# Turning the first block's results per row tile, moving its own normalised rows, and cutting the warm-up products

## The chip, the cores and the metric

One core of one Trainium2 chip. The metric is the device time of one execution in microseconds (us), lowest is best. Each kernel is run several times; the median is quoted, and for comparisons the mean against the runs of the kernel before taken in the same rounds. Profiled executions come with a trace: TensorE products (PE), weight loads (PEld), VectorE (DVE), ScalarE (ACT), GpSimd (POOL), and the sync engine's queue (SPq), which issues most transfers.

## The reference, cut to what matters

```
xn = layernorm(x)                            # 2048 rows of 640
s  = attention(xn @ wq, k_cache, v_cache) @ wo
g  = silu( (sigmoid(xn @ w_gate) * (xn @ w_up)) @ w_down )     # 640 -> 1536 -> 640
out = x + s * g
```

The change lies in the part that makes `g`, in the first of four blocks of 512 rows. It touches no arithmetic.

## The kernel before

A block is four row tiles of 128 rows. The first block is done differently from the other three: as no data has arrived, it starts from single row tiles. Row tiles are centred, turned by TensorE itself, multiplied with the gate and up weights in three groups of 512 columns (`fg`), and the products end up in `h_row`, rows on partitions. The down projection wants them the other way round, in `hT`; four DMA transposes ("turns") do that.

```
        def norm_first(t):              # the first block's properly normalised rows,
            def step():                 # wanted only by the queries, much later
                normal(t)               # VectorE, writes xn
                turn_dma(t)             # DMA transpose xnT <- xn, in the sync queue
            return step

        dummy(18)                       # 18 products of 256 columns on zeros
        dummy(6, 64)                    # 6 of 64 columns
        stats_half(0, 0)                # the first real work, once x has landed
        ...
        steps = [norm_piece(1, i) for i in range(TQ + 1)]     # rows of the second block
        steps[TQ:] = [steps[TQ]] + [norm_first(t) for t in range(TQ)]
        k = 1
        for fg in range(1, F // FT):
            for t in range(TQ):
                tile_half(t, fg, k, 0)                         # gate products
                tile_half(t, fg, k, 1)                         # up products
                tile_gated(t, fg, k, steps.pop(0) if steps else None)   # -> h_row
                k = (k + 1) % 4
        hT[0] = hpool.tile([P, NF, TB], BF16, name="hT")
        for t in range(TQ):
            nc.sync.dma_start_transpose(hT[0][:, :, t * P:(t + 1) * P], h_row[:, t, :])
        while steps:
            steps.pop(0)()
        for b in range(1, NB):
            for f in range(2):
                gated(b, f, k)
                k = (k + 1) % 4
            for q in range(TQ):
                down(b - 1, q, k)       # wants hT of row tile q
            ...
```

In the traces below, the sync queue issues its transfers in the order of the program; waits on data come on top.

The softmax here doesn't subtract the row's maximum and nothing guards it: scores larger than these inputs give would overflow.

## Time and profile before

| | kernel before |
|---|---|
| median of the 3 runs known first | 922.86 us |
| lowest, highest | 922.26, 922.90 |
| span of the profiled core | 920.8 us |
| TensorE share of the chain that ended last | 98% |

TensorE is in work for nearly all of the span, so the reader should not look at shares but at the few places where two products are further apart than one product takes. The prediction below shows the profile's lines for this. One view it tells without showing is the sync queue around the first down projection, in order of time (start in us, duration in us, engine, line, operation):

```profile
28.95 5.32 SPq L241 DMA_TRANSPOSE xnT<-xn  x3
34.32 5.12 SPq L363 DMA_TRANSPOSE hT<-h_row  x3
```

Three turns of the first block's normalised rows (xnT) come before the first turn of results (hT), though row tile 0's results were ready at 28.37 us.

### The profile page before, as it was taken

The numbers are of one execution on the slowest core, as the hardware profiler recorded it, in microseconds if no ns is written. First come the engines' busy times: TensorE is split into PE (matmuls) and PEld (weight loads), VectorE is DVE, ScalarE is ACT, GpSimd is POOL, SyncE is SP. The second block draws the span as 40 slices with busy tenths as digits, with TensorE's granted clock in tenths as the row PEclk, the third lists the DMA queues.
The fourth block names the chain that finished last, engine by engine and source line by source line (L and its number), as shares of the span: only waits on it lengthen the run. The fifth ranks groups of instructions, "written<-read, shape, count | busy, mean of one in ns | idle before, by whom it ended". The sixth has DMA issues, their size and how long they took to land.

```text
span 920.8 us, 24985 instructions
## 1 busy us (share of the span) xinstructions
PE 915.1 (99%) x11340; PEld 623.3 (68%) x11340; DVE 493.7 (54%) x989; ACT 302.3 (33%) x332; POOL 134.1 (15%) x159
## 2 busy tenths in 40 slices
PE   9999999999999999999999999999999999999998
PEld 4445455466868686767676777777776767686875
DVE  6452522445646464645555555545564646464667
ACT  4222222255142424233333333242424151515150
POOL 1000100001002000200120011001100111166733
PEclk9999999999999999999999999999999999999999
DMA  9920330115344434342525162515251615273536
GB/s 320 154 53 1 89 86 1 43 62 88 74 67 106 87 56 84 93 98 42 98 80 112 36 104 79 113 32 109 64 108 47 113 61 90 67 113 110 95 73 138
DMA packets 172107, 79.35 MB, mean 86 GB/s; under 512 B 149953, under 2 KB 167569, under 8 KB 172001
## 3 DMA queue, kind: packets, MB, share of 16 engines
q1 hardware_dynamic: 164640, 55.85, 31.7%
q0 software_dynamic: 5808, 20.52, 7.8%
q8 instruction: 88, 1.44, 0.7%
q10 hardware_dynamic: 1552, 1.39, 0.5%
q14 instruction: 19, 0.15, 0.1%
HBM read 39.45 MB, written 2.62 MB: 46 GB/s over the span
## 4 chain that ended last, share of the span: by engine, by line
PE 98%; DVE 1%; DMA 0%; SPq 0%; ACT 0%; issue 0%; DVEq 0%
PE bank L518 22%; PE bank L447 21%; PE bank L469 19%; PE bank L429 18%; PE bank L251 8%; PE bank L263 6%; PE bank L293 3%; PE bank L395 1%; PE bank L194 0%; PE bank L553 0%; DMA hT<-h_row 0%; DVE gate L504 0%; DVE o_sb L499 0%; SPq L241 0%; PE bank L235 0%; DVE h_row L303 0%
## 5 line engine op out<-in xcount | busy, mean ns | idle before, releaser
L433 ACT ACTIVATE E<-bank 128x1024 bf16<-128x1024 f32 x256 | 255.3, 1022 | 456.7 <-PE bank L429 456.6
L447 PE MATMUL bank<-xnT,wq_sb 64*128 64x512 bf16 x1800 | 226.4, 376 | 0.0
L518 PE MATMUL bank<-wo_sb,oT 64*128 64x320 bf16 x2688 | 205.2, 296 | 0.0
L429 PE MATMUL bank<-qT,kT 64*128 64x512 bf16 x1536 | 200.7, 376 | 0.0
L469 PE MATMUL bank<-vbuf,E 64*128 64x193 bf16 x4096 | 195.3, 243 | 0.1
L469 PEld LDWEIGHTS <-E 64*128 64x128 bf16 x4096 | 178.8, 94 | 10.5 <-issue 0.7
L518 PEld LDWEIGHTS <-oT 64*128 64x128 bf16 (+1 forms) x2892 | 163.2, 94 | 30.7 <-issue 0.3
L454 DVE CAST qT<-bank 128x1024 bf16<-128x1024 f32 x90 | 110.2, 1224 | 128.5 <-PE bank L447 128.5
L447 PEld LDWEIGHTS <-wq_sb 64*128 64x128 bf16 x1800 | 106.1, 100 | 87.0 <-issue 0.4
L429 PEld LDWEIGHTS <-kT 64*128 64x128 bf16 x1536 | 88.2, 94 | 73.5
L482 DVE TENSOR_TENSOR o_st<-bank,rden 128x768 bf16<-128x768 f32 x128 | 122.5, 957 | 4.4
L533 DVE TENSOR_TENSOR acc<-bank,acc 128x640 f32<-128x640 f32 x96 | 79.0, 823 | 20.2 <-PE bank L518 20.2
L118 POOL DMA_DIRECT2D vbuf<-in_A_v_cache_dram x28 | 21.1, 753 | 310.7 <-PE bank L469 307.7
L452 DVE COPY seen<-bank 128x2 f32<-128x2 f32 x90 | 14.3, 159 | 79.1 <-PE bank L447 79.1
L481 DVE RECIPROCAL rden<-bank 128x4 f32<-128x4 f32 x128 | 23.4, 183 | 60.1 <-PE bank L469 59.1
L263 PE MATMUL bank<-wd_sb,hT 128*128 128x512 bf16 (+1 forms) x384 | 52.8, 299 | 0.5 <-DMA hT<-h_row 0.5
L263 PEld LDWEIGHTS <-hT 128*128 128x128 bf16 x384 | 29.6, 98 | 23.9 <-DMA hT<-h_row 1.0
L257 DVE TENSOR_TENSOR hT<-bank,sig 128x512 bf16<-128x512 f32 x36 | 24.8, 690 | 38.2 <-ACT sig L254 38.2
L251 PE MATMUL bank<-xnT,wg_sb 128*128 128x512 bf16 x180 | 44.7, 379 | 0.0
L251 PE MATMUL bank<-xnT,wu_sb 128*128 128x512 bf16 x180 | 44.7, 379 | 0.0
L254 ACT ACTIVATE sig<-bank 128x512 bf16<-128x512 f32 x36 | 21.5, 597 | 55.8 <-PE bank L251 52.7
L97 POOL DMA_DIRECT2D wq_sb<-in_A_wq_dram x7 | 6.3, 900 | 210.5 <-PE bank L447 210.5
(51 smaller groups left out, 408.4 us busy)
## 6 DMA issues: line engine op xcount, KB each, us to landing
wo_sb<-in_A_wo_dram SPq DMA_DIRECT2D x7, 960.0 KB, 5.6
wq_sb<-in_A_wq_dram POOLq DMA_DIRECT2D x7, 960.0 KB, 6.0
k_st<-in_A_k_cache_dram POOLq DMA_DIRECT2D x14, 384.0 KB, 5.4
vbuf<-in_A_v_cache_dram POOLq DMA_DIRECT2D x28, 192.0 KB, 3.4
row<-in_A_x_dram POOLq DMA_DIRECT2D x16, 160.0 KB, 3.4
oT<-o_st SPq DMA_TRANSPOSE x128, 3.5
x_sb<-in_A_x_dram SPq DMA_DIRECT2D x3, 640.0 KB, 9.5
wd_sb<-in_B_w_down_dram SPq DMA_DIRECT2D x1, 1920.0 KB, 14.0
```

Of the source, the lines that this page charges most:

```text
L251: nc.tensor.matmul(bank[k][:, half, 0:r1 - r0], lhsT=w[:, c, f * P:(f + 1) * P], rhs=xnT[:, b, c, r0:r1], start=(c == 0), stop=(c == NCD - 1))
L257: nc.vector.tensor_tensor(hT[b][:, f, r0:r1], bank[k][:, 1, 0:r1 - r0], sig[:, 0:r1 - r0], ALU.mult)
L263: nc.tensor.matmul(wide(k)[:, d0:d1], lhsT=hT[b][:, f, q * P:(q + 1) * P], rhs=wd_sb[:, f, d0:d1], start=(f == 0), stop=(f == NF - 1))
L293: nc.tensor.matmul(bank[k][:, half, :], lhsT=xcT[:, c, t * P:(t + 1) * P], rhs=w[:, c, fg * FT:(fg + 1) * FT], start=(c == 0), stop=(c == ...
L429: nc.tensor.matmul(bank[k][:, i, :], lhsT=kT[r, pr, j, c * P:(c + 1) * P], rhs=q[r, pr * DJ + j, :], start=(j == 0), stop=(j == DJ - 1))
L433: nc.scalar.activation(E[u, pr][:, c, :, :], bank[k][:], AF.Exp, scale=scale_qk)
L447: nc.tensor.matmul(bank[k][:, half, :], lhsT=wq[r, c, col:col + DJ * (P - 1) + 1:DJ], rhs=xnT[r, b, c, :], start=(c == 0 and not second), ...
L454: nc.vector.tensor_copy(qT[u][:, 2 * m:2 * m + 2, :], bank[k][:])
L469: nc.tensor.matmul(o4[:, q, 0:DH + 1], lhsT=e[r, c, h % 2, q * P:(q + 1) * P], rhs=vbuf[r, h, c, 0:DH + 1], start=(turn == 0 and qq == 0 a ...
L482: nc.vector.tensor_tensor(o_st[u][:, :, h * DH:(h + 1) * DH], o4[:, :, 0:DH], rden[:].to_broadcast([P, TQ, DH]), ALU.mult)
L518: nc.tensor.matmul(res[:, half, :], lhsT=oT[u][r, cc, q * P:(q + 1) * P], rhs=wo[r, cc, half * HD:(half + 1) * HD], start=(turn == 0 and c ...
L533: nc.vector.tensor_tensor(cols(acc[:, t, :]), res, cols(acc[:, t, :]), ALU.add)
```

## The change

Its intent: let the first down projection find its operand in place, and let the first real products start sooner.

```diff
-        dummy(18)
-        dummy(6, 64)
+        dummy(17)
...
-        steps[TQ:] = [steps[TQ]] + [norm_first(t) for t in range(TQ)]
+        hT[0] = hpool.tile([P, NF, TB], BF16, name="hT")
...
                 tile_gated(t, fg, k, steps.pop(0) if steps else None)
                 k = (k + 1) % 4
-        hT[0] = hpool.tile([P, NF, TB], BF16, name="hT")
-        for t in range(TQ):
-            nc.sync.dma_start_transpose(hT[0][:, :, t * P:(t + 1) * P], h_row[:, t, :])
-        while steps:
-            steps.pop(0)()
+                if fg == F // FT - 1:
+                    nc.sync.dma_start_transpose(hT[0][:, :, t * P:(t + 1) * P], h_row[:, t, :])
...
-                gated(b, f, k)
+                gated(b, f, k, norm_first(f) if b == 1 else None)
...
-                gated(b, f, k, norm_piece(b + 1, f - 4) if b + 1 < NB and f >= 4 else None)
+                between = norm_first(f) if b == 1 and f < TQ else None
+                if b + 1 < NB and f >= 4:
+                    between = norm_piece(b + 1, f - 4)
+                gated(b, f, k, between)
```

## The prediction

> **What bounds the kernel now.** I read the page first: its head, its busy line, and its chain of work that ended last.
>
> ```profile
> span 920.8 us, 24985 instructions
> ...
> PE 915.1 (99%) x11340; PEld 623.3 (68%) x11340; DVE 493.7 (54%) x989; ACT 302.3 (33%) x332; POOL 134.1 (15%) x159
> ...
> PE 98%; DVE 1%; DMA 0%; SPq 0%; ACT 0%; issue 0%; DVEq 0%
> ```
>
> The tensor engine carries 98% of the chain. No other engine is near it, so only two things can shorten this program: less work on that engine, or fewer stretches in which it stands still. The change touches neither the mathematics nor the later 880 us, so I looked for standing time. The view of who waited for whom, cut to the tensor engine, has three entries for the whole program:
>
> ```profile
> PE bank L194 <- DVE warm L169: 1.1, 1, 1.1
> PE bank L263 <- DMA hT<-h_row: 0.5, 1, 0.5
> PE bank L293 <- ACT xnT L237: 0.2, 1, 0.2
> ```
>
> The first is the start of the program, which stays. The second is the one wait the change aims at: the first down projection (L263) waits for the turned results of the first block (hT). The 0.5 us is counted from the modelled end of the product before; products follow each other at 0.216 us and overlap. The last up product starts at 37.27 us by the trace's start times and the first down product at 38.20, so the step is 0.92 us where 0.216 would do: the true loss is **0.71 us**. The chain in order of time, cut to 25 to 45 us, shows what made it:
>
> ```profile
> 31.21 0.70 ACT sig L300
> 31.91 0.02 issue
> 31.93 0.75 DVE h_row L303
> 32.68 0.37 DVE xn L218
> 33.05 0.02 issue
> 33.07 1.20 SPq L241
> 34.27 0.05 issue
> 34.32 3.83 DMA hT<-h_row
> 38.15 0.05 issue
> 38.20 6.91 PE bank L263 x49
> ```
>
> Columns are start, duration, what. The reader is to see that the turn of the first row tile was not waiting for its own data. It stood in the sync queue behind a turn of normalised rows (L241), which itself waited for VectorE to write those rows (L218) at 32.68. Then issue to landing takes 3.83 us.
>
> Last, the beginning, tensor engine alone:
>
> ```profile
> 3.59 1.81 PE L194 MATMUL bank<-warm 128*128 128x256 bf16 x12
> 5.21 0.51 PE L235 MATMUL bank<-ident,xn 128*128 128x128 bf16 x3
> 5.88 0.57 PE L293 MATMUL bank<-wg_sb,xnT 128*128 128x512 bf16 x1 [0.16 <-ACT xnT L237]
> 6.28 0.28 PE L235 MATMUL bank<-ident,xn 128*128 128x128 bf16 x2
> 6.39 1.24 PE L293 MATMUL bank<-wg_sb,xnT 128*128 128x512 bf16 x4
> 7.47 0.44 PE L235 MATMUL bank<-ident,xn 128*128 128x128 bf16 x5
> 7.75 0.81 PE L293 MATMUL bank<-wu_sb,xnT 128*128 128x512 bf16 x3
> ```
>
> The warm-up products (L194) run until the first real transpose at 5.21, but VectorE had the first 128 columns of centred row 0 ready at 4.35 + 0.26 = 4.61 us (its timeline). So the transpose waited about 0.6 us behind warm-up products that were queued ahead of it.
>
> **What the Trainium skill says.** "TensorE: Matmul & The Clock Gate", Part 1 (The HAM clock gate), says the array starts at half clock and needs a window of some 3.4 us of activity to get the full one, the window running freely against the kernel. The trace agrees about the half clock: warm-up products of 256 columns start 0.213 us apart, later ones of 512 columns 0.216 us apart, and the first gate product took 0.567 us where later ones take 0.379. By these durations the change came at about 6.2 us here, in spite of 18 + 6 warm-up products. The page's PEclk row doesn't show it. "Perfetto Trace Analysis", Identifying the Most-Contended Engine, warns that matmul busy share overstates how near a kernel is to its limit; so I used start-to-start gaps, not the 99%. "DMA: Bandwidth & Descriptors", Rules for kernel authors, advises issuing a transfer early and waiting late; the 3.83 us above, exposed only because issued late, agrees. The same page (Silent corruption: two transposing streams in flight at once) forbids transposes from two queues; all stay on sync, so no serialising wait is added. No run here shows that corruption.
>
> **The change, part by part.**
>
> *Turning each row tile when done.* No turn is added or removed: 4 of hT before and after. In the kernel before, the last group of columns of row tile 0 is written by VectorE (L303) at 27.62 + 0.75 = 28.37 us, of tiles 1, 2 and 3 at 30.5, 32.7 and 34.8. The order of the sync queue in the changed build is: four turns of the second block's rows, then the four hT turns, then the first block's normalised rows. The fourth of the former is issued at 27.66 and takes 1.2 us or so, so tile 0's turn can be issued at about 28.9 and, with 3.8 us to landing, be there at 32.7, against the 37.49 us at which the down projection could start. That is 4.8 us to spare. Tile 3 is issued at about 36.6 (tiles queue 1.8 us apart) and lands near 42.3 even at 5.7 us, the slowest of the four in the view of that tile, and is wanted only after three down projections of 3.3 us each, at about 47.4. **Gain 0.71 us**, all on the path.
>
> *Moving the four normalised rows.* Four VectorE operations of 0.44 us (L218) and four turns go from the last tiles into the first four gate groups of the second block. Nothing reads these rows until the query products (L395), over 100 us later. There VectorE has one product of 0.69 us in each 2.16 us group, so 0.44 more fits (1.13 of 2.16), with four banks rotating. **0 us.**
>
> *Warm-up products.* 17 of 256 columns in place of 18 of 256 and 6 of 64: 0.213 + 6 x 0.0535 = 0.53 us fewer at the head of the queue. The 17th ends its slot at 4.66, just after the 4.61 above. The first transpose moves from 5.21 to about 4.68. ScalarE's copy follows its end (0.30 us) and takes 0.28, so the first gate product goes from 5.88 to about 5.34. From there the trace's half clock counts: if the full clock still comes at 6.2, the transposes of chunks 3 and 4 start at 5.34 + 0.43 = 5.77 instead of 6.28, their copy (0.38 us) ends at about 6.6 rather than 6.97, and the fourth product starts at about 6.65 rather than 7.03: 0.38 us. If the full clock comes by 5.3, the whole 0.54. From there the engine runs in close order and the shift is carried to the end. I take **0.43 us**.
>
> Sum: 0.71 + 0.43 = 1.14 us, 922.86 - 1.14 = 921.7 us.
>
> **Rivals.** *The weights aren't there.* The DMA engines are full in these first microseconds, and an earlier tensor engine may only meet a transfer instead. Issue plus time to landing: first gate weights 1.18 + 4.1 = 5.28 us, wanted at 5.34; first up weights 2.13 + 5.0 = 7.13, wanted at 7.2 to 7.4 instead of 7.75; the other two up chunks 3.17 + 5.2 = 8.37, wanted at 9.0. All just in time. With transfers 0.3 us later the start would gain only 0.15: 922.0.
> *The clock comes later.* With less activity early, the full clock could slip by up to a window. Each 512-column product then takes 0.427 us (twice 0.213) instead of 0.216; a slip of 3.4 us, the skill's figure, costs half, an estimated 1.7 us: 923.4. Against it: only 0.53 us of work leaves, and real transposes and products move into that time. I give it one chance in ten. An earlier clock, by the same free window, is the lucky side: some 0.5 us better.
> *The wait moves.* The second block's gate products might wait if hT turns delayed its rows; but those four turns are ahead in the queue. Turns could slow each other: the DMA row of the first 45 us is at its 9s during the four hT turns. Spread over eight microseconds they have more room, and 4.8 us to spare. Value 922.4 if a wait of that size came back; unlikely.
> *Later slack swallows it.* The whole rest has two steps above 0.26 us between products (at 177 and 883 us), so nothing there waits on a fixed time.
>
> **Range and chances.** The three runs before spread 0.64 us. The start gives -0.4 to +0.6 on my sum in ordinary cases, the clock up to 1.7 in a rare one. Range 920.8 to 922.7. Two per cent is 18 us, out of reach of anything here but another state of the chip: faster 0.005, same 0.99, slower 0.005.
>
> **What would show it.** Right: no tensor wait on hT in the wait view, a step of 0.22 us before the first down product, no L303, L218 or sync pieces in the chain at 31 to 38 us; 11333 tensor products (7 fewer); first transpose near 4.7, first gate product near 5.3, the fourth near 6.65; everything after 40 us earlier by 1.1. Wrong: a first gate product later than 5.6 or a wait on the up weights (DMA rival); 0.567-like durations after 7 us (clock rival); a new wait at L251 near 33 us or at L263 near 38 (wait moved).

## The result and the profile after

The changed kernel took 921.75 us (median of 4 runs, 921.03 to 922.59), the kernel before 922.68 us (median of 4). A ratio here is the mean time of one kernel's fast runs over that of the other's of the same rounds, so not quite the ratio of the medians: 0.9991, with a 95% interval of 0.9973 to 1.0008. This interval holds 1, so these runs alone do not prove a gain. The same kernel in five more runs beside nine of the kernel before (run e8) gave 921.77 against 922.87 us, ratio 0.9987, interval 0.9974 to 0.9999. The predicted time was 921.7.

The traces say more than so small a difference of times can. The page of the changed kernel:

```profile
span 919.2 us, 24974 instructions
...
PE 914.1 (99%) x11333; PEld 622.8 (68%) x11333; DVE 492.5 (54%) x989; ACT 302.3 (33%) x332; POOL 134.6 (15%) x159
...
PE 99%; DMA 1%; DVE 0%; SPq 0%; DVEq 0%; issue 0%
```

Seven products fewer (x11333), VectorE and ScalarE with the same number of instructions, and ScalarE gone from the chain. Who waited for whom, TensorE alone (waiter, what it waited for: us in total, times, longest):

```profile
PE bank L194 <- DVE warm L169: 1.1, 1, 1.1
PE bank L293 <- DMA wg_sb<-in_B_w_gate_dram: 0.2, 1, 0.2
```

The wait of the down projection (L263) for hT is gone. A wait for the first gate weights has come in its place at the very start; the kernel before had there a wait for ScalarE's copy. The chain in order of time, 25 to 45 us:

```profile
24.95 7.77 PE bank L293 x36
32.72 4.32 PE bank L251 x20
37.04 8.09 PE bank L263 x59
```

Three pieces of products and nothing between, where the kernel before had ScalarE, VectorE, the sync queue and a transfer. The sync queue in the changed kernel:

```profile
25.24 3.54 SPq L241 DMA_TRANSPOSE xnT<-xn  x2
28.87 6.99 SPq L361 DMA_TRANSPOSE hT<-h_row  x4
35.95 2.87 SPq L241 DMA_TRANSPOSE xnT<-xn  x2
```

The first hT turn goes out at 28.87 us instead of 34.32. By the start times, the first down product now starts 0.216 us after the product before it, where it was 0.924: 0.708 us won. The beginning, TensorE alone:

```profile
4.54 0.48 PE L235 MATMUL bank<-ident,xn 128*128 128x128 bf16 x3
5.21 0.38 PE L293 MATMUL bank<-wg_sb,xnT 128*128 128x512 bf16 x1 [0.19 <-DMA wg_sb<-in_B_w_gate_dram]
5.43 0.27 PE L235 MATMUL bank<-ident,xn 128*128 128x128 bf16 x2
5.54 1.24 PE L293 MATMUL bank<-wg_sb,xnT 128*128 128x512 bf16 x4
6.62 0.44 PE L235 MATMUL bank<-ident,xn 128*128 128x128 bf16 x5
7.14 0.81 PE L293 MATMUL bank<-wu_sb,xnT 128*128 128x512 bf16 x3
```

The first transpose moved from 5.21 to 4.54 us, the first up product (last line) from 7.75 to 7.14: 0.61 us won in this execution. But it was an execution in which everything went well: the first gate product took 0.38 us, so the full clock was there already (the warm-up products turned from 0.213 us apart to 0.11 apart at about 4.1 us). And the chain of this start no longer comes from the tensor engine:

```profile
2.13 4.96 DMA wu_sb<-in_B_w_up_dram
7.10 0.04 issue
7.14 2.53 PE bank L293 x11
```

The first up product waited for its weights, which landed at 7.10 us. So two questions were left: is each of the two gains what it seems, and what sets the start of the program?

### The profile page after: what moved, and what is told of

Read it like the earlier page. It is cut to its first block, busy times and chain, and to the rows that moved or that the text cites. A ratio compares the mean times of both kernels' runs of the same rounds, so it can differ in the third digit from the quotient of the medians.

```text
span 919.2 us, 24974 instructions
## 1 busy us (share of the span) xinstructions
PE 914.1 (99%) x11333; PEld 622.8 (68%) x11333; DVE 492.5 (54%) x989; ACT 302.3 (33%) x332; POOL 134.6 (15%) x159
## 4 chain that ended last, share of the span: by engine, by line
PE 99%; DMA 1%; DVE 0%; SPq 0%; DVEq 0%; issue 0%
PE bank L517 22%; PE bank L446 21%; PE bank L468 19%; PE bank L428 18%; PE bank L251 8%; PE bank L263 6%; PE bank L293 3%; PE bank L394 1%; DMA wu_sb<-in_B_w_up_dram 1%; PE bank L552 0%; DVE o_sb L498 0%; DVE gate L503 0%; SPq L162 0%; PE bank L235 0%; SPq L167 0%; DVEq L654 0%
## 5 line engine op out<-in xcount | busy, mean ns | idle before, releaser
L263 PE MATMUL bank<-wd_sb,hT 128*128 128x512 bf16 (+1 forms) x384 | 52.8, 299 | 0.0
L263 PEld LDWEIGHTS <-hT 128*128 128x128 bf16 x384 | 29.7, 98 | 23.1
```

Source lines behind the costliest of these rows:

```text
L263: nc.tensor.matmul(wide(k)[:, d0:d1], lhsT=hT[b][:, f, q * P:(q + 1) * P], rhs=wd_sb[:, f, d0:d1], start=(f == 0), stop=(f == NF - 1))
```

## The experiments

The theory: (1) the down projection's wait came only from the order in the sync queue, and its removal is worth 0.71 us; (2) fewer warm-up products start the real ones sooner, by 0.36 to 0.6 us depending on when the full clock comes and on the weights. Rivals: the VectorE work of the moved rows is what cost; the weights swallow the start's gain; the clock comes later with fewer warm-up products.

The first four runs went together, beside nine runs of the kernel before (mean 922.42 us); e8 to e11 went together beside nine others (mean 922.88 us).

**e1: only the rows moved and the turns early.** Against the changed kernel:

```diff
-        dummy(17)
+        dummy(18)
+        dummy(6, 64)
```

> The changed kernel with the warm-up products of the kernel before (18 of 256 columns, 6 of 64). My theory: the wait of the first down projection (0.71 us, a step of 0.92 us before it where 0.216 would do) goes away whole, the start stays, so the time is 0.6 to 0.8 us below the kernel before, and the first down product follows the last up product at 0.22 us. Rival A (all the gain is at the start): within 0.1 us of before. Rival B (the profile's other step, 0.24 us at 883 us, belongs to the change): 0.95 us below.

Measured: 921.75 us median, mean 921.71, 0.71 us below its kernel before. The ratio's interval, 0.998 to 1.0008, holds 1; single runs spread too much for five of them to prove this. The trace settles it: between the first up product and the 45th microsecond this kernel gains 0.706 us on the kernel before, all of it in one step, at the first down product. No wait on hT is left. Theory 1 holds in size, and rival A falls. Rival B is not decided by this run, whose trace lacks the step near 883 us too; it falls with e9, e10 and look e13 b below, in which the rows are moved and steps of 0.34 us or more are there (at 876 to 882 us).

A variant in which the turns stay after the loop, as in the kernel before, and only the rows are moved, was built but not run: its instructions on every engine and in the sync queue are the same as those of e1, in the same order. So of the two edits that make this gain, moving the rows out of the way is enough; where the program says "turn" changes nothing then.

**e4: only the turns early, rows left in place.** In the kernel before:

```diff
                 tile_gated(t, fg, k, steps.pop(0) if steps else None)
                 k = (k + 1) % 4
+                if fg == F // FT - 1:
+                    nc.sync.dma_start_transpose(hT[0][:, :, t * P:(t + 1) * P], h_row[:, t, :])
```

> The kernel before with one thing changed: each hT turn is put into the sync queue just behind its own row tile, between the turns of the first block's normalised rows, which stay where they were. My theory (the first hT turn was late only because three turns of normalised rows stood ahead of it): its first hT turn is issued near 28.9 us instead of 34.3, and the gain is the same 0.6 to 0.8 us as with the rows moved away. Rival (the VectorE work of the rows in that stretch is itself what costs): the gain is half or less.

Measured: 922.01 us median, mean 921.86, 0.56 below its kernel before (interval of the ratio 0.9982 to 1.0007). The sync queue now alternates:

```profile
29.25 1.45 SPq L363 DMA_TRANSPOSE hT<-h_row  x1
30.79 1.55 SPq L241 DMA_TRANSPOSE xnT<-xn  x1
32.44 1.47 SPq L363 DMA_TRANSPOSE hT<-h_row  x1
33.99 1.55 SPq L241 DMA_TRANSPOSE xnT<-xn  x1
```

VectorE has exactly the instructions of the kernel before, in its order, and yet the step at the first down product is gone: 0.706 us in the trace again. So the rival (VectorE's work costs) falls, and the queue order is shown to be the cause: either edit alone removes the wait.

**e2: only fewer warm-up products.** In the kernel before:

```diff
-        dummy(18)
-        dummy(6, 64)
+        dummy(17)
```

> The kernel before with only the warm-up products changed (17 of 256 columns). My theory: first transpose near 4.6 us instead of 5.2, first gate product near 5.2 to 5.35, a gain of 0.36 us when the full clock comes at 6.2 us or so and 0.55 to 0.6 us when it comes by 5; the step of 0.92 us at the first down product stays. Rival A: nothing, the weights' landing swallows it. Rival B (clock comes later with less activity): first gate products of 0.567 us or longer after 6.5 us and a time equal to or above before.

Measured: 922.08 us median, mean 922.12, 0.30 below its kernel before (interval 0.9985 to 1.001). The wait on hT is there, and the start is earlier:

```profile
PE bank L194 <- DVE warm L169: 1.1, 1, 1.1
PE bank L263 <- DMA hT<-h_row: 0.6, 1, 0.6
PE bank L293 <- DMA wg_sb<-in_B_w_gate_dram: 0.2, 1, 0.2
```

```profile
4.66 0.53 PE L235 MATMUL bank<-ident,xn 128*128 128x128 bf16 x3
5.45 0.58 PE L293 MATMUL bank<-wg_sb,xnT 128*128 128x512 bf16 x1 [0.25 <-DMA wg_sb<-in_B_w_gate_dram]
5.83 0.42 PE L235 MATMUL bank<-ident,xn 128*128 128x128 bf16 x2
6.04 1.28 PE L293 MATMUL bank<-wg_sb,xnT 128*128 128x512 bf16 x4
7.16 0.44 PE L235 MATMUL bank<-ident,xn 128*128 128x128 bf16 x5
7.44 0.81 PE L293 MATMUL bank<-wu_sb,xnT 128*128 128x512 bf16 x3
```

First transpose 0.55 us earlier, first up product (7.44 against 7.75) 0.31 earlier: a quarter of a microsecond went to the gate weights, which had not landed, and to products at half clock. The two parts alone sum to 0.71 + 0.30 = 1.01 us of mean time; the whole change measured 1.06 (9 runs of it, 13 of the kernel before, in the same rounds). They add up within the spread of the runs (the five of e1 lie 0.81 us apart, the five of e2 0.47), which is no sharp test; 0.30 us of mean time is not clear of noise by itself, and the earlier start rests on the traces.

**e7: the first up weights from the other queue.** Against the changed kernel, after the finding that its start hangs on this transfer:

```diff
         load_f(nc.scalar, wg_sb, wg_r, 0, 4, 0, 3)
+        load_f(nc.scalar, wu_sb, wu_r, 0, 4, 0, 3)
         load_f(nc.sync, wg_sb, wg_r, 0, 4, 3, NCD)
-        load_f(nc.sync, wu_sb, wu_r, 0, 4, 0, 3)
```

> The changed kernel with the first three chunks of up weights issued from ScalarE's queue right behind the gate weights (near 1.7 us) instead of from the sync queue (2.1 us). In the changed kernel's profile the chain starts with this transfer, which ends at 7.10 us; the product waiting for it could have started at 6.90. My theory: if the issue time sets the landing, it lands 0.3 to 0.5 us earlier, the chain starts elsewhere and 0.2 us are gained in executions with an early clock, none with a late one. Rival (the transfer is bound by the bytes ahead of it): landing unchanged within 0.1 us, same time; the gate chunks 3 and 4 may come later and cost 0.1 to 0.5.

A miss: 923.26 us median, 1.37 us above its kernel before in the mean (ratio 1.0016, interval 1.0003 to 1.0028); by medians it is 0.79, as one of the five runs took 926.14 us. The chain at the start of this run:

```profile
1.66 6.00 DMA wg_sb<-in_B_w_gate_dram
7.66 0.04 issue
```

Gate chunks 3 and 4, issued at 1.66 us as ever, now took 6.00 us to land instead of 4.3, and the fourth gate product waited 1.3 us for them. The moved load itself, issued at 1.67 us instead of 2.13, took 6.9 us instead of 5.0, so it landed later and not earlier. The expectation named the risk for the gate chunks but put it at 0.5 us at most. So an earlier issue did not bring the data earlier here; that the transfers slowed each other by sharing the DMA engines fits this, but is argued. This start does not explain the whole 1.37 us: at 45 us this run is 1.43 us behind the first profile of the changed kernel, but only 0.10 behind the profile of the kernel before, which had the hT wait. A further 0.81 us was added in its last 45 us.

**e8: the changed kernel again; e9, e10, e11: 24, 13 and no warm-up products.** Against the changed kernel:

```diff
-        dummy(17)
+        dummy(24)        # e9;  13 in e10, 0 in e11
```

> The changed kernel unaltered, to learn how much of its spread (921.03 to 922.59 us in four runs) is the moment at which the full tensor clock comes. My theory: the time follows that moment: an execution whose warm-up products turn from 0.213 us spacing to 0.108 before the first gate product reads near 921.1, one whose products stay at the half clock until 6 us or later reads 922 or more. Rival: the spread is made in the last 45 us, where three of the six profiles so far have a step of 0.38 to 0.77 us between tensor products near 877 to 884 us and three have none.

> The changed kernel with 24 full warm-up products in place of 17: 7 x 0.213 = 1.49 us more at the head of the queue when cold, less if the clock comes among them. My theory (warm-up products still queued when the first row is ready delay everything one for one): first transpose at 5.2 to 6.2 us instead of 4.6, time 0.5 to 1.2 us above the changed kernel. Rival (the start is bound by the weights anyway): no more than 0.2 us above.

> The changed kernel with 13 warm-up products, which end near 3.83 us when cold, 0.7 us before the first transpose's data. My theory: no gain over 17, as the first transpose waits for VectorE at about 4.6 us either way; first transpose 4.5 to 4.65 us; time within 0.3 us of the changed kernel. Rival (the clock comes later with less activity): half-clock products of 0.5 us or longer still seen after 7 us and 0.3 to 1.2 us more time.

> The changed kernel with no warm-up products at all. First transpose still at about 4.6 us. Theory: the half clock then lasts until some 3 to 7 us after that, so 512-column products are 0.427 us apart instead of 0.216 until 8 to 11 us, and the time is 1 to 3 us above the changed kernel. Rival (warm-up products are of no use here, the loads bound the first 10 us anyway): within 0.3 us.

Medians: 17 products 921.77 us (mean 921.72), 24 products 922.44 (922.43), 13 products 922.80 (922.61), none 923.32 (923.12). So 24 cost 0.7 us over 17, as the theory of the queue said; but 13 cost 0.9 and none 1.4, so there the clock rival is the better one. (Five runs of one kernel lie 1.05 to 1.83 us apart here, so 24 and 13 are not told apart.) The single profile of e10 did not show why: it happened to be its fastest run, with the full clock by 4.7 us. In e8 the up weights came late. The first up product started at 7.86 us, and the waits of TensorE read:

```profile
PE bank L293 <- DMA wu_sb<-in_B_w_up_dram: 0.3, 1, 0.3
```

Its expectation (the clock sets the time, and a late one reads 922 or more) was thus too narrow; its full clock came at 6.3 us. The landing of the same transfer differed between two executions of the same kernel, 7.10 and 7.82 us.

**e12 and e13: more looks, to catch slow executions.** Two more profiles each of the kernels with 13 and with 17 products. They were run on another chip. (The one run of the kernel before in this round took 921.92 us, less than any in the other rounds; one run says little, but the changed kernel's looks, 921.32 and 921.69, are only 0.60 and 0.23 below it.)

> 13 warm-up products again, for its profile alone: its timed runs were 0.8 to 1.0 us slower on average than with 17, but the one profile of it was of an early clock and its fastest run. Theory: a look at 922.6 us or more shows the clock coming late (first gate product 0.5 us or longer, half-clock products after 7 us). Rival: a slow look shows the same early clock, and the time lies in the last 45 us or in a late landing of the up weights.

> The same again, as the moment of the clock differs between executions. Same expectation: with the clock by 5 us the first up product starts near 7.1 us, with the clock after 7 us near 8 us or later, and the difference is carried whole to the end.

> The changed kernel again for its profile. Of its two profiles one had the full clock at 4.1 us and the first up weights at 7.1, the other 6.3 and 7.8 us. Theory: each execution's start of the first up product is the later of two things, the clock-set arrival of the tensor engine (6.9 to 7.3 us) and the landing of these weights (7.1 to 7.8), and a look near 921.1 has both early. Rival: the landing is the same in all and only the clock differs.

> The same again. Over the looks, the time less the start of the first up product (less any step near 880 us) should be constant within 0.1 us.

Both looks at 13 products were slow (922.70 and 923.06 us) and show the clock. The second one's start, TensorE alone:

```profile
4.61 0.59 PE L235 MATMUL bank<-ident,xn 128*128 128x128 bf16 x3 [0.60 <-DVE xn L227]
5.27 0.61 PE L293 MATMUL bank<-wg_sb,xnT 128*128 128x512 bf16 x1
5.67 0.42 PE L235 MATMUL bank<-ident,xn 128*128 128x128 bf16 x2
5.88 1.91 PE L293 MATMUL bank<-wg_sb,xnT 128*128 128x512 bf16 x4
7.59 0.74 PE L235 MATMUL bank<-ident,xn 128*128 128x128 bf16 x5
8.12 1.49 PE L293 MATMUL bank<-wu_sb,xnT 128*128 128x512 bf16 x3
```

The bracket in the first line is an idle stretch of the tensor engine: 13 products end too soon, and it waits 0.60 us for VectorE. Four gate products then take 1.91 us instead of 1.24: half clock, and it lasted until 10.0 us (9.3 in the other look). That the idle stretch delayed the clock is not shown: fewer products and the idle stretch came together, the profile of e10 had the same stretch (0.7 us) and the full clock at 4.7 us, and with no warm-up product at all (e11) it came at 8.4.

The looks at the changed kernel show that the clock and the weights each can set the start. In e13 a the clock was late (6.6 us) and the waits show no weights: first up product at 7.42 us. In e13 b the clock was early (4.1 us), but TensorE waited 0.2 us for gate and 0.2 us for up weights: 7.44 us. The expectation of a constant time after the first up product, less any late step, held within 0.03 us for the four profiles of the changed kernel.

All profiles together, from the traces' start times; "lag" is the delay of the same product against the first profile of the changed kernel, at 45 us; the column after it is what was added to that delay from 875 us to the last product:

| execution | warm-up products | full clock from, us | first transpose | first up product | lag at 45 us | added in the last 45 us | time of this run |
|---|---|---|---|---|---|---|---|
| before | 18 + 6 | 6.3 | 5.21 | 7.75 | 1.33 | 0.25 | 922.62 |
| e1 | 18 + 6 | 5.1 | 5.16 | 7.45 | 0.31 | 0.05 | 921.39 |
| e4 | 18 + 6 | 6.7 | 5.21 | 7.89 | 0.76 | 0.22 | 922.02 |
| e9 | 24 | 4.8 | 5.52 | 7.80 | 0.67 | 0.30 | 922.00 |
| after | 17 | 4.1 | 4.54 | 7.14 | 0 | 0 | 921.03 |
| e2 (hT wait kept) | 17 | 6.2 | 4.66 | 7.44 | 1.05 | 0.34 | 922.42 |
| e8 | 17 | 6.3 | 4.66 | 7.86 | 0.72 | 0 | 921.77 |
| e13 a | 17 | 6.6 | 4.66 | 7.42 | 0.28 | 0 | 921.32 |
| e13 b | 17 | 4.1 | 4.58 | 7.45 | 0.30 | 0.36 | 921.69 |
| e10 | 13 | 4.7 | 4.69 | 7.10 | -0.04 | 0.54 | 921.53 |
| e12 a | 13 | 9.3 | 4.64 | 8.31 | 1.65 | 0 | 922.70 |
| e12 b | 13 | 10.0 | 4.61 | 8.12 | 1.94 | 0 | 923.06 |
| e11 | none | 8.4 | 4.60 | 8.11 | 1.15 | 0 | 922.18 |
| e7 (up weights moved) | 17 | 5.6 | 4.66 | 8.57 | 1.43 | 0.81 | 923.26 |

Add the two columns of delay to 921.03 and the time of each run comes out within 0.02 us (for the kernel before: 921.03 + 1.33 + 0.25 = 922.61), but for e12 b. From 45 to 875 us all executions take the same time within 0.01 us; only e12 b takes 0.07 us more, added near 210 us. So nearly all that differs, between kernels and between executions of one kernel, is made in the first 38 and the last 45 us. In the first, four things set it: the warm-up products still queued (e9, with an early clock and no wait for weights, lags by 0.67), the moment of the clock, the landing of the first weights, and the hT wait. The last column differs between executions of one kernel (0 and 0.36 in two looks at the changed one), and kernels with and without the change have it. But the three profiles with the rows left in place (before, e2, e4) all have it, and of the eleven with the rows moved only four have 0.3 us or more; whether the change makes it rarer is open. (The expectation of e8 counts such steps in three of the first six profiles; the traces have them in four: before, e2, e4 and e7.) In look e13 b it fell where a VectorE operation of the last rows (L503) took 1.50 us, against 1.10 in look e13 a, and a POOL one ran beside it; that the two disturbed each other is argued only, and no experiment was made of it.

By the distance from its own kernel before, no kernel beat the changed one: e7 was the attempt, and more or fewer warm-up products were both slower.

## Why the prediction was right, point by point

- **The turns (0.71 us): right, in size and cause.** Measured 0.708 us between the two kernels and 0.706 in both e1 and e4. The first turn went out at 28.87 us (28.9 predicted), and landed 3.9 to 4.2 us later. The fourth was issued at 34.3, not at 36.6: turns in this stretch took 1.4 to 1.9 us each, none piled up, and it went out when its own tile was ready (34.23). The prediction's own times, 28.9 and three turns of 1.8 us, or tile 3 ready at 34.8, give less than 36.6 too. Of the 3.83 us from issue to landing, which the prediction calls exposed, only 0.71 were lost time. The prediction did not see that either of the two edits alone would do.
- **The moved rows (0 us): right.** The step between products in the second block stays at 0.216 us.
- **The warm-up products (0.43 us taken, 0.38 to 0.54 given): a mechanism that was right, and a size that was somewhat high.** e2 measured 0.30 us in the mean, its trace 0.31. The best profile gave 0.61, but it had the clock at 4.1 us and the kernel before at 6.3; against e1, which kept the old warm-up products and had it at 5.1, it is 0.31 again. The first gate product near 5.34 us was met (5.18 to 5.45 in five profiles). What failed is the step "all just in time": it took one profile's landing times for constants. The up weights, taken to land at 7.13 us, landed at 7.10 in one profile and at 7.82 in another. The DMA rival ("the weights aren't there"), valued at 922.0, was thus true in part.
- **The clock rival**, given one chance in ten: at 17 products it did not happen, five profiles having the full clock by 4.1 to 6.6 us, as with 18 + 6 (5.1 to 6.7). At 13 it happened in two profiles of three, and the half clock lasted to 9.3 and 10.0 us. The predicted cost of half the slip came out well: against look e13 a (clock at 6.6 us, lag 0.28) the clock was 2.7 and 3.4 us later, and the lag 1.37 and 1.66 us more. The margin was narrower than the prediction knew.
- **The sum and the range:** 1.14 us predicted; 0.93 between medians and 1.06 in means of more runs. That the measured median lies within 0.05 us of the predicted time is luck: the four runs spread over 1.56 us, and the start gave less than was predicted. That a run can move by half a microsecond in its last 45 us was not in the prediction; its range covered it.

## What to carry to other kernels

In a queue that serves in order, an urgent transfer waits for the data of whatever stands ahead of it (34.32 us instead of 28.87 here): when an operand is late, look at what was issued before it, not only at who made it, and put work that nobody wants yet behind it. In this kernel the warm-up work did best when it ended just as the first data was ready: more of it stood in the way (24 products cost 0.7 us), and with less the engine idled and in most executions stayed at half clock longer (13 cost 0.9). For effects below the spread of single runs, compare start times in the trace stretch by stretch, and take several profiles of the same kernel before calling a landing time a constant.

## What the Trainium skill lacked or had wrong

- "TensorE: Matmul & The Clock Gate", Part 1, puts the change to full clock at about 4 us of sustained activity, give or take 0.5 us, and a budget of about 3.4 us. Here the first product ran at 1.06 us, and with 17 or more products the full clock came at 4.1 to 6.7 us, 3.0 to 5.7 us later (with idle stretches of up to 0.3 us on the way); with 13 products and an idle stretch of 0.6 to 0.7 us behind them, at 4.7, 9.3 and 10.0 us in three profiles. How much an idle stretch shorter than a window may delay the clock isn't stated, and these runs don't separate it from the smaller number of products.
- The same page, Part 4 (PE-mode transpose), says that transposes take about 275 ns in one kernel and that the full clock does not engage for them. The transposes of this kernel (products with the identity, L235) took 0.219 us, 0.056 apart, after the change of clock, and 0.314 us, 0.107 apart, before it, so they follow the clock (the durations have modelled ends; the distances are between starts). They ran among ordinary products, so nothing is shown of transposes alone, and the profile doesn't show whether they use the engine's transpose mode.
- "DMA: Bandwidth & Descriptors", Issuing engines are not separate DMA queues, says that transfers from several issuing engines interleave on the same DMA engines and that issuing from several only saves the sequencer's time. It gives no figure for what that can cost: in e7, with one load moved to the other queue and issued 0.46 us earlier, that load took 6.9 us instead of 5.0 from its issue and another one 6.00 instead of 4.3.
- No page that bears on this says how far the landing of one and the same transfer varies between executions: here 7.10 and 7.82 us, enough to swallow the gain of an earlier start.
